# Which bursts of a unit hand a quarter of their exps to VectorE: 0, 2, 4, 6 in place of 1, 3, 5, 7

## The chip, the cores and the metric

The kernel runs on one core of a Trainium2 chip. The metric is the device time of one execution in microseconds; lower is better. The engines are called TensorE (PE in the profile, its weight loads PEld), ScalarE (ACT), VectorE (DVE), GpSimd (POOL) and SyncE (SP, which issues most DMAs).

## What is computed

Two branches over 2048 tokens of 1024 features, mixed by a gate for each token:

```python
g = sigmoid((A_x * gate_w).sum(-1, keepdims=True))
a = ssm(A_x)      # h_t = Lam_bar * h_(t-1) + B_bar x_t, complex; y = 2 Re(C h) + Dskip * x
b = mha(A_x)      # 32 heads of 32: softmax(q k^T / sqrt(32)) v, then @ wo
return g * a + (1 - g) * b
```

The attention branch takes 32 x 2048 x 2048 = 134 million exps, and these are what ScalarE does nearly all the time.

## The kernel before

The attention is cut into 512 **bursts**. A group is four heads (8 groups), a unit is 256 queries of a group (8 units a group), and a burst is 256 keys of a unit (8 bursts a unit, numbered 0 to 7). Bursts are also numbered through, from 0 to 511; burst 481 is burst 1 of unit 60.

In a burst TensorE makes the scores of four heads in PSUM (`burst`, L1575): eight matmuls, two PSUM slots of two banks each, out of three slots that rotate. The first slot holds heads 0 and 1, the second heads 2 and 3. ScalarE then runs one exp a slot, 128x1024 into a bf16 tile (L1593). Two bursts later TensorE multiplies these tiles with V (`pv`, L1649: 16 small matmuls a burst), which add up in bank 6 over a whole unit. With burst 1 of the next unit the sum is complete; VectorE divides by the row sums (`normalize`, L1662 and L1663) and a DMA transposes the result.

Everything else is poured into the bursts by hand-written rules in `build`: **dense chains** on TensorE of four matmuls a burst into bank 7. These are the projections of the next group (`proj`, `vproj`; L1402, L1420), the inputs of the state-space branch (`u`; L1432), its outputs (`c`; L1461 with a small diagonal matmul L1467 after every four), and at the end the output projection (`out`; L1492). When a chain is done, VectorE evacuates bank 7 (L1409, L1426, L1438, L1474, L1498). The next chain can't start before that, so in the burst in which a chain ends the value matmuls are placed behind the dense ones, except where the unit's sum is completed. VectorE also runs the scans and products of the state-space branch (L1340, L1349) in what time `build` reckons is left of each burst (`dve_t`, `limit`, `period`).

In some half-units **VectorE takes a quarter of the second slot's exps**: a pair of bursts of a half-unit, 256 columns each (the last head's scores for the second 128 keys). In a burst of a pair VectorE reads the columns at once, scales them to a fixed-point power of two and stores them as integers (x_in, L1584). ScalarE's second exp is then 128x768 (L1590); it is issued only after x_in is done, since the two share a bank. When both bursts of a pair are read, three steps on VectorE (x_q, L1614, L1615, L1611) work out a cubic for the fraction, and one on POOL (L1612) writes the bf16 bits, xp. TensorE multiplies xp with V in four small matmuls (`x_pv`, L1629), and the value group of such a burst has 14 matmuls instead of 16.

`X_PLAN` lists the half-units that have a pair, by the number of their first burst, and `X_AT` says which two bursts of a half-unit form it. `x_plan` (L1595) sets when L1629 is issued: in burst 6 for a pair of the first half, in burst 1 of the next unit for one of the second half, just ahead of that unit's `normalize`. In `build` the pair is planned at the half-unit's first burst (L1738); steps of an earlier pair that are left are put out before x_in of a new one (L1740), and the steps come ahead of other background work on VectorE. All queues run in the order in which `build` records their instructions.

The launch ends in a tail in which the last unit is finished without overlap.

Of the kernel before, what the change touches and what calls it, by code (L numbers as in the profile page):

```python
# [931 lines left out]
RING = 60  # L932
C_LOADS = 28

X_AT = ((1, 3), (5, 7))
X_PLAN = (144, 148, 152, 156, 160, 164, 168, 172, 176, 180, 184, 188, 192, 196, 200, 204, 208, 212, 216, 220, 224, 228, 232, 236, 240, 244, 248, 252, 256, 260, 296, 300, 304, 308, 312, 316, 320, 324, 352, 360, 364, 368, 372, 376, 380, 392, 396, 400, 404, 408, 412, 416, 420, 424, 428, 432, 436, 440, 444, 448, 452, 456, 460, 464, 468, 472, 476, 480, 484, 488, 492, 496, 500)
X_COLS = 256
X_A = SCALE * math.log2(math.e) * 65536.0
X_LO = -127.0 * 65536.0
# [14 lines left out]
class FastPath:  # L954
# [722 lines left out]
    def build(self):  # L1677
# [54 lines left out]
        for p in range(first, NBURST):  # L1732
# [3 lines left out]
            if p > first:  # L1736
                t0 += period
            if p % 4 == 0 and p in X_PLAN:  # L1738
                self.x_plan(p // 8, X_AT[p // 4 % 2])
            while p in self.x_of and len(self.xbg) > 1:  # L1740
# [315 lines left out]
```

## Time and profile before

| | |
|---|---|
| median of 3 runs | 944.16 us (943.36 to 944.33) |
| the profiled execution | 945.17 us, its span 943.3 us |
| TensorE busy | 912.6 us (97%), weight loads 506.8 us (54%) |
| ScalarE busy | 919.3 us (97%) |
| VectorE busy | 714.6 us (76%) |
| GpSimd busy | 57.1 us (6%) |
| mean granted TensorE clock | 0.996 |
| bursts with an exp on VectorE | 146 (73 pairs) |

Rows of a timeline give the start in us, the time in us, the engine, the line, the operation, what it writes and reads, and how many instructions of the kind were merged; in brackets, how long the engine sat idle before and what ended it. A row of the waits gives the waiting instruction, what it waited for, the sum in us, how often, and the longest. A unit of eight bursts lasts some 14 us.

### The profile page before, as it was taken

The numbers are of one execution on the slowest core, as the hardware profiler recorded it, in microseconds if no ns is written. First come the engines' busy times: TensorE is split into PE (matmuls) and PEld (weight loads), VectorE is DVE, ScalarE is ACT, GpSimd is POOL, SyncE is SP. The second block draws the span as 40 slices with busy tenths as digits, with TensorE's granted clock in tenths as the row PEclk, the third lists the DMA queues.
The fourth block names the chain that finished last, engine by engine and source line by source line (L and its number), as shares of the span: only waits on it lengthen the run. The fifth ranks groups of instructions, "written<-read, shape, count | busy, mean of one in ns | idle before, by whom it ended". The sixth has DMA issues, their size and how long they took to land.

```text
span 943.3 us, 33875 instructions
## 1 busy us (share of the span) xinstructions
PE 912.6 (97%) x15316; PEld 506.8 (54%) x15316; DVE 714.6 (76%) x1462; ACT 919.3 (97%) x1034; POOL 57.1 (6%) x113
## 2 busy tenths in 40 slices
PE   8899999999999999999999999999999999999996
PEld 4555644565455565455655555544655655554553
DVE  2788888899888888885679965468989755576664
ACT  6999999999999999999999999999999999999996
POOL 2000000000000001010010010000000001001000
PEclk9999999999999999999999999999999999999998
DMA  9559533310123002121022401124101111424312
GB/s 197 96 105 133 75 55 78 77 31 26 41 64 94 19 8 50 41 72 42 8 38 53 85 16 41 41 61 97 42 16 41 42 38 52 151 85 122 116 61 73
DMA packets 157093, 60.90 MB, mean 65 GB/s; under 512 B 145680, under 2 KB 145680, under 8 KB 156944
## 3 DMA queue, kind: packets, MB, share of 16 engines
q1 hardware_dynamic: 154784, 58.16, 27.7%
q8 instruction: 121, 1.98, 0.9%
q10 hardware_dynamic: 2160, 0.53, 0.3%
q14 instruction: 28, 0.23, 0.1%
HBM read 16.79 MB, written 12.58 MB: 31 GB/s over the span
## 4 chain that ended last, share of the span: by engine, by line
ACT 48%; PE 42%; DVE 5%; POOL 1%; SPq 1%; DMA 1%; issue 1%; DVEq 0%
ACT f_pt L1593 40%; PE f_ps L1649 9%; PE f_ps L1461 9%; PE f_ps L1575 8%; PE f_ps L1402 4%; PE f_ps L1492 4%; PE f_ps L1420 3%; ACT f_OT L1593 2%; PE f_ps L1432 2%; ACT f_Et L1593 2%; ACT f_cT_re L1593 2%; ACT f_cT_im L1593 2%; ACT f_pt L1590 1%; DVE f_xq L1611 1%; POOL f_xp L1612 1%; DVE f_xq L1615 1%
## 5 line engine op out<-in xcount | busy, mean ns | idle before, releaser
L1593 ACT ACTIVATE f_pt<-f_ps 128x1024 bf16<-128x1024 f32 x798 | 753.9, 1138 | 8.4 <-PE f_ps L1575 7.0
L1649 PEld LDWEIGHTS f_ps<-f_V,f_pt 128*128 128x128 bf16 x7260 | 223.9, 96 | 95.6 <-issue 67.9
L1649 PE MATMUL f_ps<-f_V,f_pt 128*128 128x33 bf16 x7260 | 259.8, 178 | 0.0
L1575 PE MATMUL f_ps<-f_Q,f_K 32*128 32x256 bf16 x4096 | 203.5, 273 | 13.9 <-ACT f_pt L1593 2.8
L1575 PEld LDWEIGHTS f_ps<-f_Q,f_K 32*128 32x128 bf16 x4096 | 60.8, 92 | 153.1 <-ACT f_pt L1593 119.9
L1584 DVE TENSOR_SCALAR f_xi<-f_ps 128x256 int32<-128x256 f32 x146 | 61.8, 424 | 101.7 <-PE f_ps L1575 99.0
L1432 PE MATMUL f_ps<-f_xT,f_wb 128*128 128x512 bf16 x512 | 131.4, 378 | 0.6 <-DVE f_pf L1223 0.4
L1590 ACT ACTIVATE f_pt<-f_ps 128x768 bf16<-128x768 f32 x146 | 125.2, 857 | 0.0
L1402 PE MATMUL f_ps<-f_xT,f_wb 128*128 128x512 bf16 x464 | 119.4, 379 | 0.0
L1612 POOL TENSOR_SCALAR f_xp<-f_xq 128x512 int16<-128x512 f32 x73 | 47.7, 654 | 629.3 <-DVE f_xq L1611 629.3
L1349 DVE TENSOR_TENSOR_SCAN f_ht<-f_pf,f_init,f_ut 128x512 bf16<-128x512 f32 x64 | 80.5, 1273 | 0.0
L1461 PE MATMUL f_ps<-f_cT_re,f_hp 128*128 128x512 bf16 x192 | 72.7, 379 | 0.0
L1461 PE MATMUL f_ps<-f_cT_im,f_hp 128*128 128x512 bf16 x192 | 72.6, 378 | 0.0
L1492 PE MATMUL f_ps<-f_wb,f_OT 128*128 128x512 bf16 x220 | 62.9, 381 | 0.1
L1432 PEld LDWEIGHTS f_ps<-f_xT,f_wb 128*128 128x128 bf16 x512 | 40.1, 96 | 39.2 <-issue 7.8
L1420 PE MATMUL f_ps<-f_wb,f_xT 128*128 128x128 bf16 x896 | 59.3, 219 | 0.0
L1402 PEld LDWEIGHTS f_ps<-f_xT,f_wb 128*128 128x128 bf16 x464 | 36.1, 96 | 36.5 <-issue 8.2
L1420 PEld LDWEIGHTS f_ps<-f_wb,f_xT 128*128 128x128 bf16 x896 | 50.4, 97 | 3.8 <-issue 3.6
L1611 DVE SCALAR_TENSOR_TENSOR f_xq<-f_xi,f_xq 128x512 f32<-128x512 int16 x73 | 50.5, 692 | 2.5
L1614 DVE SCALAR_TENSOR_TENSOR f_xq<-f_xi 128x512 f32<-128x512 uint16 x73 | 50.4, 690 | 2.0
L1615 DVE SCALAR_TENSOR_TENSOR f_xq<-f_xq,f_xi 128x512 f32<-128x512 f32 x73 | 50.0, 685 | 0.9
L1438 DVE CAST f_ub<-f_ps 128x512 bf16<-128x512 f32 x48 | 33.1, 690 | 15.5 <-PE f_ps L1432 15.2
(147 smaller groups left out, 841.6 us busy)
## 6 DMA issues: line engine op xcount, KB each, us to landing
ag_scratch<-f_Ag SPq DMA_DIRECT2D x32, 256.0 KB, 2.2
f_hp<-ag_scratch SPq DMA_DIRECT2D x32, 256.0 KB, 2.9
f_wb<-in_B_wqkv_dram SPq DMA_DIRECT2D x21, 256.0 KB, 4.0
out_dram<-f_xT SPq DMA_DIRECT2D x16, 256.0 KB, 2.2
f_wb<-in_B_wo_dram SPq DMA_DIRECT2D x2, 768.0 KB, 6.1
f_OT<-f_On SPq DMA_TRANSPOSE x63, 2.3
f_wb<-in_B_wqkv_dram ACTq DMA_DIRECT2D x2, 256.0 KB, 4.1
f_wb<-in_A_B_re_dram SPq DMA_TRANSPOSE x32, 3.4
```

The source lines that it names most:

```text
L1349: ops.append((1.29, lambda ri=ri: dve(lambda e: e.tensor_tensor_scan(ht[:, ri, :], rr, ut[:, ri, :], self.init[:, ri, j:j + 1], ALU.mult, ...
L1402: mms.append((1, lambda e, f, l, a=a: e.matmul(ps[:, bank, :], w[:, g % 2, part, a, :], xT[:, a, 512 * ch:512 * (ch + 1)], start=f, stop=l ...
L1420: m = e.matmul(ps[:, bank, 128 * q:128 * (q + 1)], xT[:, a, 128 * kt:128 * (kt + 1)], w[:, g % 2, 2, a, :], start=(a == 0), stop=(a == 7))
L1432: mms.append((1, lambda e, f, l, a=a: e.matmul(ps[:, 7, :], bT[:, (2 * n + ri) % 3, a, :], xT[:, a, 512 * ch:512 * (ch + 1)], start=f, sto ...
L1461: mms.append((1, lambda e, f, l, j=j, ri=ri: e.matmul(ps[:, 7, :], hp[:, ri, j, cols], cT[ri][:, j, 512 * cb:512 * (cb + 1)], start=f, sto ...
L1492: mms.append((1, lambda e, f, l, j=j: e.matmul(ps[:, 7, :], OT[:, j, 256 * qb + 128 * r:256 * qb + 128 * (r + 1)], wo[j][0][:, 512 * cb:51 ...
L1575: m = e.matmul(ps[:, 2 * sl[h // 2] + h % 2, 256 * kl:256 * (kl + 1)], K[32 * h:32 * h + 32, g % 2, 128 * kt:128 * (kt + 1)], Q[32 * h:32 ...
L1584: first = self.dve(lambda e: e.tensor_scalar(self.xi[:, X_COLS * n:X_COLS * (n + 1)], ps[:, 2 * s + 1, 512 - X_COLS:512], X_A, X_LO, ALU.m ...
L1590: self.S.op("act", lambda e, s=s, p=p: e.activation(flat(self.tile[p]), flat(ps[:, 2 * s:2 * s + 2, :]), ACT.Exp, scale=SCALE), reads=[("S ...
L1593: self.act(lambda e, s=s, p=p: e.activation(self.tile[p], ps[:, 2 * s:2 * s + 2, :], ACT.Exp, scale=SCALE), [("S", s)], [("pt", p)], "exp")
L1611: self.dve(lambda e: e.scalar_tensor_tensor(xq[:], hi, 128.0 / X_K, xq[:], ALU.mult, ALU.add), i2 + ["xq"], ["xq"], "x_q")
L1649: m = e.matmul(ps[:, 6, o:o + 33], self.tile[p][:, h2, 256 * kl + 128 * qt:256 * kl + 128 * (qt + 1)], V[:, g % 2, 2 * i + kl, h, :], star ...
```

## The change

The pairs of a half-unit are bursts 0 and 2, or 4 and 6, instead of 1 and 3, or 5 and 7. The list of half-units is drawn anew by the same rule: 144, 352 and 376 drop out, 328 and 332 come in, so 72 pairs are left of 73.

```diff
-X_AT = ((1, 3), (5, 7))
-X_PLAN = (144, 148, 152, ..., 320, 324, 352, 360, 364, 368, 372, 376, 380, 392, ..., 500)
+X_AT = ((0, 2), (4, 6))
+X_PLAN = (148, 152, ..., 320, 324, 328, 332, 360, 364, 368, 372, 380, 392, ..., 500)
```

No other line changes. L1596, by which L1629 is issued in burst 6 or in burst 1 of the next unit, stays as it is. What `build` records changes with the two tables: x_in, the shorter exps and the 14-matmul value groups move by one burst. Around them the order on VectorE changes. Of the 73 last x_q steps before, 62 were followed at once by the next x_in; of the 72 after, 13 are, and 52 are followed by the evacuation of a dense chain. C chains shift by two bursts around bursts 198 and 402, and with them their stores.

More of the change, by code (lines that the diff above doesn't have):

```diff
@@ L933 @@
 C_LOADS = 28
-X_AT = ((1, 3), (5, 7))
-X_PLAN = (144, 148, 152, 156, 160, 164, 168, 172, 176, 180, 184, 188, 192, 196, 200, 204, 208, 212, 216, 220, 224, 228, 232, 236, 240, 244, 248, 252, 256, 260, 296, 300, 304, 308, 312, 316, 320, 324, 352, 360, 364, 368, 372, 376, 380, 392, 396, 400, 404, 408, 412, 416, 420, 424, 428, 432, 436, 440, 444, 448, 452, 456, 460, 464, 468, 472, 476, 480, 484, 488, 492, 496, 500)
+X_AT = ((0, 2), (4, 6))
+X_PLAN = (148, 152, 156, 160, 164, 168, 172, 176, 180, 184, 188, 192, 196, 200, 204, 208, 212, 216, 220, 224, 228, 232, 236, 240, 244, 248, 252, 256, 260, 296, 300, 304, 308, 312, 316, 320, 324, 328, 332, 360, 364, 368, 372, 380, 392, 396, 400, 404, 408, 412, 416, 420, 424, 428, 432, 436, 440, 444, 448, 452, 456, 460, 464, 468, 472, 476, 480, 484, 488, 492, 496, 500)
 X_COLS = 256
```

## The prediction

> **What bounds the kernel now.** I read the page first: ScalarE and TensorE are both busy 97% of the span, and the chain that ended last changes hands between them.
>
> ```profile
> span 943.3 us, 33875 instructions
> ...
> PE 912.6 (97%) x15316; PEld 506.8 (54%) x15316; DVE 714.6 (76%) x1462; ACT 919.3 (97%) x1034; POOL 57.1 (6%) x113
> ...
> ACT 48%; PE 42%; DVE 5%; POOL 1%; SPq 1%; DMA 1%; issue 1%; DVEq 0%
> ```
>
> So the stages have to be told apart. In a burst without an exp on VectorE the score matmuls (L1575) start 1.83 us apart and are released by ScalarE, here in the timeline of the weight loads:
>
> ```profile
> 507.06 0.12 PEld L1575 LDWEIGHTS f_ps<-f_Q,f_K 32*128 32x128 bf16 x8 [0.56 <-ACT f_pt L1593]
> 508.89 0.12 PEld L1575 LDWEIGHTS f_ps<-f_Q,f_K 32*128 32x128 bf16 x8 [0.55 <-ACT f_pt L1593]
> ```
>
> The same timeline of unit 60 (bursts 480 to 487, VectorE's exps in 481, 483, 485 and 487), one L1575 row a burst, and two rows of ScalarE in it:
>
> ```profile
> 876.33 0.12 PEld L1575 LDWEIGHTS f_ps<-f_Q,f_K 32*128 32x128 bf16 x8
> 876.65 0.47 PEld L1649 LDWEIGHTS f_ps<-f_V,f_pt 128*128 128x128 bf16 x16 [0.21 <-issue]
> ...
> 878.03 0.12 PEld L1575 LDWEIGHTS f_ps<-f_Q,f_K 32*128 32x128 bf16 x8 [0.42 <-ACT f_pt L1593]
> 878.36 0.41 PEld L1649 LDWEIGHTS f_ps<-f_V,f_pt 128*128 128x128 bf16 x14 [0.21 <-issue]
> 879.02 0.17 PEld L1629 LDWEIGHTS f_ps<-f_V,f_xp 128*128 128x128 bf16 x4 [0.25 <-POOL f_xp L1612]
> ...
> 880.10 0.12 PEld L1575 LDWEIGHTS f_ps<-f_Q,f_K 32*128 32x128 bf16 x8 [0.42 <-ACT f_pt L1593]
> ...
> 881.98 0.12 PEld L1575 LDWEIGHTS f_ps<-f_Q,f_K 32*128 32x128 bf16 x8 [0.42 <-ACT f_pt L1593]
> ...
> 883.62 0.12 PEld L1575 LDWEIGHTS f_ps<-f_Q,f_K 32*128 32x128 bf16 x8
> ...
> 885.32 0.12 PEld L1575 LDWEIGHTS f_ps<-f_Q,f_K 32*128 32x128 bf16 x8 [0.42 <-ACT f_pt L1593]
> ...
> 886.98 0.12 PEld L1575 LDWEIGHTS f_ps<-f_Q,f_K 32*128 32x128 bf16 x8
> ...
> 888.79 0.12 PEld L1575 LDWEIGHTS f_ps<-f_Q,f_K 32*128 32x128 bf16 x8 [0.42 <-ACT f_pt L1593]
> ...
> 890.43 0.12 PEld L1575 LDWEIGHTS f_ps<-f_Q,f_K 32*128 32x128 bf16 x8
> ```
>
> ```profile
> 876.10 0.88 ACT L1590 ACTIVATE f_pt<-f_ps 128x768 bf16<-128x768 f32 x1
> ...
> 879.51 0.92 ACT L1590 ACTIVATE f_pt<-f_ps 128x768 bf16<-128x768 f32 x1
> 880.55 2.91 ACT L1593 ACTIVATE f_pt<-f_ps 128x1024 bf16<-128x1024 f32 x3
> ```
>
> The bursts last 1.70, 2.07, 1.88, 1.64, 1.70, 1.66, 1.81 and 1.64 us, 14.10 in all. Their differences are TensorE's work: 16 value matmuls against 14 cost 0.06 (rows 0.47 and 0.41), the matmuls on xp (L1629) 0.10. The gap of 0.42 before L1575 is the same wherever a dense chain's matmuls stand in front, so I read it as TensorE's own and not as ScalarE's. Two bursts stand out. Burst 1 (2.07) has less work than burst 6 (1.81) and is longer: in it L1629 waits 0.25 us for POOL's xp. Burst 2 (1.88) waits for the bank of the chain that ended in burst 1. ScalarE needs 3.41 us for three long exps and a short one (876.10 to 879.51, so 0.91 and 0.69 each), 13.6 a unit; it is within reach but not the limit. After the wait it idles: the short exp at 879.51 is followed only 1.04 later.
>
> The view of waits gives the sum of this wait; the timeline of VectorE and TensorE in burst 151 to 153 shows one of the long ones:
>
> ```profile
> PEld f_ps L1629 <- POOL f_xp L1612: 8.7, 22, 0.8
> ...
> PE f_ps L1629 <- POOL f_xp L1612: 5.2, 11, 0.7
> ```
>
> ```profile
> 287.78 0.40 PE L1575 MATMUL f_ps<-f_Q,f_K 32*128 32x256 bf16 x8
> ...
> 291.18 0.40 PE L1575 MATMUL f_ps<-f_Q,f_K 32*128 32x256 bf16 x8
> ...
> 292.68 0.27 PE L1629 MATMUL f_ps<-f_V,f_xp 128*128 128x33 bf16 x4 [0.66 <-POOL f_xp L1612]
> ...
> 293.81 0.40 PE L1575 MATMUL f_ps<-f_Q,f_K 32*128 32x256 bf16 x8
> ```
>
> ```profile
> 288.29 0.42 DVE L1584 TENSOR_SCALAR f_xi<-f_ps 128x256 int32<-128x256 f32 x1
> 289.18 0.69 DVE L1438 CAST f_OT<-f_ps 128x512 bf16<-128x512 f32 x1 [0.47 <-PE f_ps L1432]
> 289.79 0.68 DVE L1614 SCALAR_TENSOR_TENSOR f_xq<-f_xi 128x512 f32<-128x512 uint16 x1
> 290.50 0.69 DVE L1615 SCALAR_TENSOR_TENSOR f_xq<-f_xq,f_xi 128x512 f32<-128x512 f32 x1
> 291.23 0.69 DVE L1611 SCALAR_TENSOR_TENSOR f_xq<-f_xi,f_xq 128x512 f32<-128x512 int16 x1
> 292.01 0.62 POOL L1612 TENSOR_SCALAR f_xp<-f_xq 128x512 int16<-128x512 f32 x1 [6.22 <-DVE f_xq L1611]
> ```
>
> The second pair of a unit is read in burst 7, its three steps come after that burst's evacuation, and TensorE wants xp in burst 1 of the next unit: xp was there 4.9 us after burst 7's L1575 (287.78 to 292.68), and was wanted at 291.18 + 0.74 (the place of L1629 behind L1575 in burst 1, from 878.03 to 879.02 less its wait), 4.1 after it.
>
> **The change, part by part.** *Pairs one burst earlier, wanted when they were.* The offsets 6 and 9 in L1596 stay. From the rows: x_in starts 0.5 after L1575 and takes 0.42; the three steps follow at 0.71, 0.73 and 0.78; POOL takes 0.62 and L1629 starts 0.05 later: 3.8 us when nothing stands between. From burst 6's L1575 to the want is 1.81 + 1.64 + 1.70 + 0.74 = 5.9. So 2.1 us are left, and an evacuation (0.69) or a slow POOL (row below, 1.52) fits in them. The first pair gains a burst on a slack that already sufficed. All waits on xp go. Their worth: burst by burst, burst 1's length less that of the same work without the wait. The first is 2.63 (291.18 to 293.81) less 1.81 for its C work, 0.82; unit 60 gives 2.07 less 1.75 (burst 6 with 14 value matmuls), 0.32; the last (505) is another 0.32. There are 36 such bursts, 12.3 us together; the two rows of waits say 13.9, the upper end. I take **-12.3**.
>
> ```profile
> 406.95 1.52 POOL L1612 TENSOR_SCALAR f_xp<-f_xq 128x512 int16<-128x512 f32 x1 [5.10 <-DVE f_xq L1611]
> ```
>
> *The short value group moves into a covered burst.* Groups of 14 stood in bursts 1, 3, 5, 7; now in 0, 2, 4, 6. Burst 2 ends a fixed time after the evacuation of burst 1's chain, however short its value group: 0.06 is lost a unit. With 29 units whose chain ends in burst 1: **+1.6**.
>
> *Dense chains.* The recording's VectorE budget puts C chains two bursts off around bursts 198 and 402, so that more of them end in burst 1. The price of such an end, from the timeline:
>
> ```profile
> 565.14 0.40 PE L1575 MATMUL f_ps<-f_Q,f_K 32*128 32x256 bf16 x8
> ...
> 566.95 0.40 PE L1575 MATMUL f_ps<-f_Q,f_K 32*128 32x256 bf16 x8
> 567.06 0.75 DVE L1474 TENSOR_SCALAR f_Ag<-f_ps,f_gcol 128x512 f32<-128x512 f32 x1 [0.25 <-PE f_ps L1461]
> 567.40 2.96 ACT L1593 ACTIVATE f_pt<-f_ps 128x1024 bf16<-128x1024 f32 x3
> 567.87 0.39 PE L1461 MATMUL f_ps<-f_cT_re,f_hp 128*128 128x512 bf16 x1
> ...
> 568.89 0.40 PE L1575 MATMUL f_ps<-f_Q,f_K 32*128 32x256 bf16 x8
> ```
>
> Burst 2 then lasts 1.94 (566.95 to 568.89) instead of 1.76 with 16 value matmuls; four more of these make 4 x 0.18 = **+0.7**. The chain's store to scratch moves with it on SP's queue, past stores and transposes; the buffers are double and the stores are read far later, so it costs nothing.
>
> *One pair fewer* (bursts 144, 352 and 376 lose theirs, 328 and 332 gain one). Four plain bursts take 7.33; with a pair 6.81 (883.62 to 890.43), or 7.02 with the longer C work: **+0.4**. VectorE loses 2.9 us of work and POOL 0.6, both beside other work.
>
> *Where plain bursts follow.* Four of the 36 waits lie in half-units that stay or become plain, where ScalarE's 1.83 would take back part of what they free: of 1.7 us I put **+0.6**.
>
> *x_in behind the evacuation.* In the recorded order x_in stood behind the last x_q in 62 of 146 cases; now it stands behind an evacuation in 117 of 144. The worst case is the one above: the evacuation ends at 567.81, 0.86 after L1575, x_in would end at 1.30, and the short exp may start 0.91 after the exp at 567.40, that is 1.36 after L1575. Elsewhere the evacuation ends 0.3 earlier. It costs nothing, by a margin of 0.06 in burst 2. Then x_in and two steps follow in burst 2 and the third in burst 3, done some 3.4 after burst 2's L1575, or 1.5 into burst 3, about when that burst's chain ends; bounds 0 and 0.1 us a unit, and I take 0 since the value matmuls behind the chain cover the evacuation.
>
> Sum: -12.3 + 1.6 + 0.7 + 0.4 + 0.6 = **-9.0 us**. The profiled execution took 945.17, so 936.2 with a span near 934.3; it was 1.0 above the median 944.16, and against that the forecast is **935.2 us**. With 13.9 gone and only the pair lost it would be 930.7, the lower bound.
>
> **The rivals.** *The two engines meet.* Without the wait a unit of such work costs TensorE about 13.8 and ScalarE 13.6. If they hold each other up by 0.06 us in each of 72 half-units, 4.3 us are lost: 939.5. For it: the margin is 0.2 a unit. Against: in bursts 483 to 487 no such loss is seen.
>
> *Slower: the short exp waits for x_in.* If evacuations end later than in the rows above, x_in passes its 1.36 and ScalarE is late in every such burst. From 0.07 us later in all 144 bursts on (9 us) it eats the gain; at 0.17 beyond the margin the time would be 935.2 + 144 x 0.1 = 949.6. For it: the 0.06 of burst 2. Against: three bursts of four have 0.3 more, and where ScalarE is a little early TensorE sets the pace.
>
> *No change: ScalarE alone sets the time,* the waits on xp are covered, and what counts is its 0.44 us for the lost pair: 944.6. The idle at 880.55 speaks against it. The Trainium skill ("Perfetto Trace Analysis", Identifying the Most-Contended Engine) would have it so: it says that matmul busy time misleads, that TensorE's headroom is judged by the weight loads' share, and that the engine of highest occupancy is the one to work on. By that, 54% against ScalarE's 97%, the change brings nothing; the spacing of unit 60's bursts, which follows TensorE's work, disagrees.
>
> **How the numbers follow.** Forecast 0.68, the engines meet 0.17, slower 0.09, no change 0.06. A difference of 0.2% (1.9 us) is about what a measurement of this kernel can tell from no change. Faster: 0.68 + 0.17 = 0.85; same 0.06; slower 0.09. The range runs from the lower bound, rounded, 931.0, to just past the case where the engines meet, 940.0.
>
> **What would show it.** Right: the rows "L1629 <- POOL" gone from the waits; burst 1 near 1.81 where it was 2.0 to 2.6; POOL's op ending in burst 0 or before; ScalarE's short exp count at 144. Wrong: waits of L1590 on VectorE's L1584; evacuations that end over 0.9 after L1575; L1575 waiting longer for ScalarE inside the pair stretches; new waits of the first dense matmul on an evacuation in bursts 0, 4 or 6.

## The result, and the profile after

The changed kernel takes 939.07 us (median of 5 runs, 938.90 to 939.55) against 944.33 us of the kernel before (5 runs, 943.36 to 944.86): a ratio of 0.9946 [0.9931, 0.9960], so 5.3 us faster. The forecast was 935.2 us, 9.0 us faster. The sign and the main mechanism came as predicted; 3.7 us of the gain did not.

The page of the changed kernel: its span, the busy times, the chain that ended last, and the two groups of ScalarE's exps (the last column is ScalarE's idle time ahead of them).

```profile
span 937.3 us, 33936 instructions
...
PE 910.5 (97%) x15316; PEld 504.8 (54%) x15316; DVE 716.6 (76%) x1457; ACT 918.4 (98%) x1034; POOL 56.0 (6%) x112
...
ACT 53%; PE 41%; DVE 3%; SPq 1%; issue 1%; DMA 1%; DVEq 0%
...
L1593 ACT ACTIVATE f_pt<-f_ps 128x1024 bf16<-128x1024 f32 x800 | 755.2, 1154 | 2.9 <-PE f_ps L1575 2.2
...
L1590 ACT ACTIVATE f_pt<-f_ps 128x768 bf16<-128x768 f32 x144 | 125.0, 868 | 0.8 <-DVE f_xi L1584 0.7
```

The profiled execution took 939.07 us, the median itself. ScalarE's busy time is what it was (919.3 before); the span around it is 6.0 us shorter. POOL, 1% of the chain before, is gone from it. The view of the waits says why:

```profile
PEld f_ps L1575 <- ACT f_pt L1593: 129.1, 334, 1.0
...
DVE f_rc L1662 <- PE f_ps L1629: 47.7, 34, 2.3
...
ACT f_pt L1590 <- DVE f_xi L1584: 0.7, 1, 0.7
```

No row "L1629 <- POOL" is left, where two stood before: 8.7 us for the weight loads, 5.2 us for the matmuls. (They don't add up to 13.9 us of waiting: the 11 waits of the second row lie in bursts that the 22 of the first have too.) VectorE's `normalize` (L1662) waits longer for the value matmuls than before (47.7 us in sum against 15.3), since its own work is done earlier. A new row has come: ScalarE's short exp (L1590) waits for x_in (L1584), once, 0.7 us. The timeline of the weight loads in unit 60, one L1575 row a burst as in the prediction:

```profile
870.61 0.12 PEld L1575 LDWEIGHTS f_ps<-f_Q,f_K 32*128 32x128 bf16 x8
870.94 0.41 PEld L1649 LDWEIGHTS f_ps<-f_V,f_pt 128*128 128x128 bf16 x14 [0.21 <-issue]
...
872.38 0.12 PEld L1575 LDWEIGHTS f_ps<-f_Q,f_K 32*128 32x128 bf16 x8 [0.54 <-ACT f_pt L1593]
872.70 0.47 PEld L1649 LDWEIGHTS f_ps<-f_V,f_pt 128*128 128x128 bf16 x16 [0.21 <-issue]
873.10 0.17 PEld L1629 LDWEIGHTS f_ps<-f_V,f_xp 128*128 128x128 bf16 x4
...
874.18 0.12 PEld L1575 LDWEIGHTS f_ps<-f_Q,f_K 32*128 32x128 bf16 x8 [0.42 <-ACT f_pt L1593]
...
876.07 0.12 PEld L1575 LDWEIGHTS f_ps<-f_Q,f_K 32*128 32x128 bf16 x8 [0.42 <-ACT f_pt L1593]
...
877.76 0.12 PEld L1575 LDWEIGHTS f_ps<-f_Q,f_K 32*128 32x128 bf16 x8
...
879.43 0.12 PEld L1575 LDWEIGHTS f_ps<-f_Q,f_K 32*128 32x128 bf16 x8 [0.44 <-ACT f_pt L1593]
...
881.12 0.12 PEld L1575 LDWEIGHTS f_ps<-f_Q,f_K 32*128 32x128 bf16 x8
...
882.88 0.12 PEld L1575 LDWEIGHTS f_ps<-f_Q,f_K 32*128 32x128 bf16 x8 [0.43 <-ACT f_pt L1593]
...
884.57 0.12 PEld L1575 LDWEIGHTS f_ps<-f_Q,f_K 32*128 32x128 bf16 x8
```

The bursts now last 1.77, 1.80, 1.89, 1.69, 1.67, 1.69, 1.76 and 1.69 us, 13.96 in all instead of 14.10. Burst 1 fell from 2.07 to 1.80, and L1629 follows the value matmuls with no idle time. But burst 0 grew from 1.70 to 1.77 although its value group is the short one now, and the gap in front of the next L1575 is 0.54 instead of 0.42. POOL's op was done 2.2 us before L1629 wanted it:

```profile
870.30 0.62 POOL L1612 TENSOR_SCALAR f_xp<-f_xq 128x512 int16<-128x512 f32 x1 [6.01 <-PE f_ps L1492]
```

**A measure for what follows.** The spacing of the L1575 rows cuts the run into bursts. All that differs between the kernels lies between L1575 of burst 144 and that of burst 508: 275.39 to 926.00 us before, 274.78 to 919.75 after, so 650.61 and 644.97 us. This stretch became 5.6 us shorter. The start of burst 144 lies between 274.40 and 275.46 in all the kernels below, with no order to it, so the 0.6 us ahead of the stretch are left out. In every profile the granted clock is 1.00 over the whole stretch, and lower behind it (0.76 in the last 17.6 us of the changed kernel), so what the clock does to the end of the launch doesn't touch this measure either. It comes from one profiled execution a kernel.

### The profile page after: what moved, and what is told of

It reads as the page before. It is cut to its first block, busy times and chain, and to the rows that moved or that the text cites. A ratio compares the mean times of both kernels' runs of the same rounds, so it can differ in the third digit from the quotient of the medians.

```text
span 937.3 us, 33936 instructions
## 1 busy us (share of the span) xinstructions
PE 910.5 (97%) x15316; PEld 504.8 (54%) x15316; DVE 716.6 (76%) x1457; ACT 918.4 (98%) x1034; POOL 56.0 (6%) x112
## 4 chain that ended last, share of the span: by engine, by line
ACT 53%; PE 41%; DVE 3%; SPq 1%; issue 1%; DMA 1%; DVEq 0%
ACT f_pt L1593 44%; PE f_ps L1649 10%; PE f_ps L1461 9%; PE f_ps L1575 8%; PE f_ps L1492 4%; PE f_ps L1402 4%; PE f_ps L1420 3%; PE f_ps L1432 2%; ACT f_OT L1593 2%; ACT f_pt L1590 2%; ACT f_Et L1593 2%; ACT f_cT_re L1593 2%; ACT f_cT_im L1593 2%; SPq L1052 1%; DVE f_Ag L1474 1%
## 5 line engine op out<-in xcount | busy, mean ns | idle before, releaser
L1593 ACT ACTIVATE f_pt<-f_ps 128x1024 bf16<-128x1024 f32 x800 | 755.2, 1154 | 2.9 <-PE f_ps L1575 2.2
L1575 PE MATMUL f_ps<-f_Q,f_K 32*128 32x256 bf16 x4096 | 203.4, 273 | 16.2 <-ACT f_pt L1593 3.3
L1575 PEld LDWEIGHTS f_ps<-f_Q,f_K 32*128 32x128 bf16 x4096 | 60.7, 92 | 158.7 <-ACT f_pt L1593 129.1
L1590 ACT ACTIVATE f_pt<-f_ps 128x768 bf16<-128x768 f32 x144 | 125.0, 868 | 0.8 <-DVE f_xi L1584 0.7
L1584 DVE TENSOR_SCALAR f_xi<-f_ps 128x256 int32<-128x256 f32 x144 | 60.7, 421 | 26.8 <-PE f_ps L1575 24.8
L1662 DVE RECIPROCAL f_rc<-f_ps 128x8 f32<-128x8 f32 x63 | 13.1, 207 | 63.8 <-PE f_ps L1629 47.7
```

The lines of the kernel that those rows point to most:

```text
L1575: m = e.matmul(ps[:, 2 * sl[h // 2] + h % 2, 256 * kl:256 * (kl + 1)], K[32 * h:32 * h + 32, g % 2, 128 * kt:128 * (kt + 1)], Q[32 * h:32 ...
L1584: first = self.dve(lambda e: e.tensor_scalar(self.xi[:, X_COLS * n:X_COLS * (n + 1)], ps[:, 2 * s + 1, 512 - X_COLS:512], X_A, X_LO, ALU.m ...
L1590: self.S.op("act", lambda e, s=s, p=p: e.activation(flat(self.tile[p]), flat(ps[:, 2 * s:2 * s + 2, :]), ACT.Exp, scale=SCALE), reads=[("S ...
L1593: self.act(lambda e, s=s, p=p: e.activation(self.tile[p], ps[:, 2 * s:2 * s + 2, :], ACT.Exp, scale=SCALE), [("S", s)], [("pt", p)], "exp")
```

## The experiments

Times are medians. The kernel before gave 943.90 us beside the first four kernels, on the same chip, and 944.18 beside the last two, on another.

### The new list alone

```diff
-X_PLAN = (144, 148, 152, ..., 324, 352, 360, 364, 368, 372, 376, 380, ..., 500)
+X_PLAN = (148, 152, ..., 324, 328, 332, 360, 364, 368, 372, 380, ..., 500)
 X_AT = ((1, 3), (5, 7))
```

> The kernel before with the changed list of 72 half-units, pairs still at 1, 3 and 5, 7. If the position is what gains: the waits of L1629 on POOL stay near 14 us and the time is that of the kernel before plus the lost pair, 944.3 + 0.4 = 944.7 (944.0 to 945.5). If the new list brings part of the gain: 942 or less.

Measured: 944.49 us, ratio 1.0004 [0.9995, 1.0013]; the stretch 650.87 us, 0.3 longer. Its waits:

```profile
PEld f_ps L1629 <- POOL f_xp L1612: 9.0, 25, 0.8
...
PE f_ps L1629 <- POOL f_xp L1612: 5.3, 15, 0.7
```

The waits on xp are all there. The gain comes from the places of the pairs, not from the list.

### No wait, nothing else moved

```diff
-            self.dve(lambda e: e.scalar_tensor_tensor(xq[:], hi, 128.0 / X_K, xq[:], ...), ..., "x_q")
...
-                (0.7, 0.0, lambda: self.dve(lambda e: e.scalar_tensor_tensor(xq[:], xq[:], E1 / E3 * w * w, lo, ...), ..., "x_q")),
+                (0.7, 0.0, lambda: None),
```

The base is the kernel before, with its pairs and its order; xp is ready two steps earlier. The edit also takes 97 us of work off VectorE (busy 618.0 us against 714.6).

> The kernel before with two of the three x_q steps (L1615, L1611) left out, the recorded order otherwise the same; the cubic is then not computed, only its first step. xp is there 1.4 us earlier and no wait in burst 1 was longer than 0.8. If those waits are what the change removes: 12.3 us less some 1.5 us that ScalarE takes back, 933.5 (932.5 to 936), with burst 1 at 1.75 to 1.81. If ScalarE alone sets the time: 944. If the waits only cost half of what the rows say: 938 to 939.

Measured: 933.73 us, ratio 0.9891 [0.9876, 0.9906]; no row "L1629 <- POOL"; the stretch 640.00 us. So the waits were worth 10.6 us (10.2 by the medians), not 12.3, if VectorE's lighter load does nothing else; the table below bears on that. The chain that ended last, on its page, and burst 0 and 1 of unit 60 in the timeline of the weight loads:

```profile
ACT 96%; SPq 1%; DVE 1%; DMA 1%; PE 1%; issue 0%; DVEq 0%
```

```profile
866.90 0.12 PEld L1575 LDWEIGHTS f_ps<-f_Q,f_K 32*128 32x128 bf16 x8
...
868.61 0.12 PEld L1575 LDWEIGHTS f_ps<-f_Q,f_K 32*128 32x128 bf16 x8 [0.42 <-ACT f_pt L1593]
...
870.36 0.12 PEld L1575 LDWEIGHTS f_ps<-f_Q,f_K 32*128 32x128 bf16 x8 [0.42 <-ACT f_pt L1593]
```

Burst 0 lasts 1.71 and burst 1 1.75 us, the number that the prediction had put for this work without the wait. ScalarE now carries 96% of the chain: without the waits the two engines stand so close that the chain runs almost wholly through ScalarE. Where the 10.6 us come from is seen when the bursts of the stretch are summed by their place in the unit (364 bursts, in us; worked out from all L1575 rows):

| burst of the unit | 0 | 1 | 2 | 3 | 4 | 5 | 6 | 7 | sum |
|---|---|---|---|---|---|---|---|---|---|
| before | 80.60 | 94.19 | 84.14 | 77.61 | 78.13 | 76.95 | 82.44 | 76.55 | 650.61 |
| without the wait | 80.54 | 82.52 | 83.79 | 78.42 | 78.33 | 77.40 | 82.43 | 76.57 | 640.00 |
| changed kernel | 80.60 | 83.57 | 85.06 | 80.83 | 77.73 | 78.04 | 80.83 | 78.31 | 644.97 |

Burst 1 gives 11.7 us, in 32 units, every one with a pair just before; no other burst gets more than 0.04 us shorter but bursts 2 and 4 of units 56 and 57, whose bursts 3 and 5 get longer by about as much. So it is the wait that counts here, not VectorE's load. About 1.1 are given back at once in bursts 2 to 5. Of these 0.7 lie in units 33, 41, 48 and 63, where plain bursts follow (unit 33: bursts 3 to 5 go from 1.69, 1.75, 1.81 to 1.83, 1.84, 1.83, ScalarE's own pace).

### The two casts put behind x_in

In the changed kernel two evacuations of the output chains (L1498) are followed by two casts on VectorE (L1504, L1505), in bursts 454 and 458, and x_in of these bursts stands behind all three. The timeline of VectorE in burst 458, then ScalarE's short exp, then the weight loads of bursts 458 to 460:

```profile
831.51 0.75 DVE L1498 SCALAR_TENSOR_TENSOR f_Et<-f_ps,f_gcol,f_hp 128x512 f32<-128x512 f32 x1
832.29 0.43 DVE L1504 CAST f_Et<-f_Et 128x512 bf16<-128x512 f32 x1
832.75 0.69 DVE L1505 TENSOR_TENSOR f_Et<-f_Et 128x512 bf16<-128x512 f32 x1
833.36 0.42 DVE L1584 TENSOR_SCALAR f_xi<-f_ps 128x256 int32<-128x256 f32 x1
```

```profile
833.82 0.81 ACT L1590 ACTIVATE f_pt<-f_ps 128x768 bf16<-128x768 f32 x1 [0.70 <-DVE f_xi L1584]
```

```profile
831.40 0.12 PEld L1575 LDWEIGHTS f_ps<-f_Q,f_K 32*128 32x128 bf16 x8 [0.42 <-ACT f_pt L1593]
...
833.28 0.12 PEld L1575 LDWEIGHTS f_ps<-f_Q,f_K 32*128 32x128 bf16 x8 [0.42 <-ACT f_pt L1593]
...
835.59 0.12 PEld L1575 LDWEIGHTS f_ps<-f_Q,f_K 32*128 32x128 bf16 x8 [0.86 <-ACT f_pt L1593]
```

x_in ends at 833.78, 2.38 us after its burst's L1575; the short exp starts 0.04 later, after 0.70 of idle time; burst 459 lasts 2.31 us. Burst 454 is the same with less: x_in ends 1.85 us after its burst's L1575. The three x_q steps that follow are late too, and with them the next evacuation, for which the first dense matmuls of bursts 456 and 460 wait. For burst 456, VectorE and the weight loads:

```profile
828.04 0.74 DVE L1498 SCALAR_TENSOR_TENSOR f_Et<-f_ps,f_gcol,f_hp 128x512 f32<-128x512 f32 x1
```

```profile
828.84 0.55 PEld L1492 LDWEIGHTS f_ps<-f_wb,f_OT 128*128 128x128 bf16 x4 [0.34 <-DVE f_Et L1498]
```

The edit puts the casts into VectorE's background work; in the trace they then come behind x_in of bursts 456 and 460:

```diff
-                    self.dve(lambda e: e.tensor_copy(hi, su), ...)
-                    self.dve(lambda e: e.tensor_tensor(lo, su, hi, ALU.subtract), ...)
+                    self.bg.append((0.45, lambda: self.dve(lambda e: e.tensor_copy(hi, su), ...), 0))
+                    self.bg.append((0.7, lambda: self.dve(lambda e: e.tensor_tensor(lo, su, hi, ALU.subtract), ...), 0))
```

> The changed kernel with the two casts of the last unit's sums (L1504, L1505) recorded as background work behind the next x_in instead of between the evacuation and x_in. If x_in late behind them is what lengthens bursts 452 to 460: the half-units from 452 to 463, now 7.11, 7.84 and 7.19, come to about 6.9 each, 1.4 us less, 937.6 (937.2 to 938.2), and the wait of L1590 on L1584 is gone. If those bursts are long for another reason (the loads of scratch, the shorter chains): 939.1.

Measured: 937.84 us, ratio 0.9936 [0.9922, 0.9949]; the stretch 643.68 us, 1.3 less than the changed kernel's. The same place, VectorE and the weight loads of bursts 458 to 460:

```profile
831.10 0.75 DVE L1498 SCALAR_TENSOR_TENSOR f_Et<-f_ps,f_gcol,f_hp 128x512 f32<-128x512 f32 x1
831.77 0.41 DVE L1584 TENSOR_SCALAR f_xi<-f_ps 128x256 int32<-128x256 f32 x1
```

```profile
831.02 0.12 PEld L1575 LDWEIGHTS f_ps<-f_Q,f_K 32*128 32x128 bf16 x8 [0.45 <-ACT f_pt L1593]
...
832.87 0.12 PEld L1575 LDWEIGHTS f_ps<-f_Q,f_K 32*128 32x128 bf16 x8 [0.42 <-ACT f_pt L1593]
...
834.47 0.12 PEld L1575 LDWEIGHTS f_ps<-f_Q,f_K 32*128 32x128 bf16 x8 [0.15 <-ACT f_pt L1593]
```

Burst 459 is 1.60 us again. The evacuation ahead of burst 456's chain starts 0.42 us before that burst's L1575, where it started 0.29 behind it, and the weight loads of bursts 456 and 460 no longer wait for it. For burst 456:

```profile
827.14 0.75 DVE L1498 SCALAR_TENSOR_TENSOR f_Et<-f_ps,f_gcol,f_hp 128x512 f32<-128x512 f32 x1
```

```profile
828.24 0.55 PEld L1492 LDWEIGHTS f_ps<-f_wb,f_OT 128*128 128x128 bf16 x4
```

The half-units that begin with bursts 452, 456 and 460 go from 7.11, 7.84 and 7.20 us to 6.91, 6.91 and 6.98, 1.35 together, and the wait of L1590 on L1584 is gone. Of these 1.35 us, 0.9 lie in bursts 455 and 459, which wait for a short exp that x_in made late: the mechanism of the slower rival, at two places. The other 0.44 lie in bursts 456 and 460, which wait for the late evacuation.

### Less for ScalarE in burst 7

```diff
+            elif z == 1 and i == 7 and B - 1 in self.x_of:
+                flat = lambda ap: ap.rearrange("p h n -> p (h n)")[:, 0:896]
+                self.act(lambda e, s=s, p=p: e.activation(flat(self.tile[p]), flat(ps[:, 2 * s:2 * s + 2, :]), ...), ...)
```

The base is the changed kernel; burst 7 is plain there, and its second exp gets 896 columns in place of 1024.

> The changed kernel with ScalarE's second exp of burst 7 cut to 896 columns in units whose second half has a pair (128 columns of exps are left out, about 0.11 us each). If ScalarE sets burst 0, which lasts 1.76 in units of 16-matmul chains where TensorE's work is 1.65: burst 0 falls to 1.65 to 1.68 there, 12 to 15 units by 0.1, 937.8 (937.3 to 938.3). If burst 0 is long for a reason on TensorE or VectorE: 939.1.

Measured: 936.91 us, ratio 0.9926 [0.9912, 0.9940]; the stretch 643.26 us, 1.7 less than the changed kernel's. That is more gain than expected: the time lies below the range. Burst 480 (burst 0 of unit 60) in the timeline of the weight loads:

```profile
869.01 0.12 PEld L1575 LDWEIGHTS f_ps<-f_Q,f_K 32*128 32x128 bf16 x8
...
870.66 0.12 PEld L1575 LDWEIGHTS f_ps<-f_Q,f_K 32*128 32x128 bf16 x8 [0.43 <-ACT f_pt L1596]
```

It lasts 1.65 us instead of 1.77, and the gap behind it is 0.43 again. Burst by burst the two kernels differ in burst 0 of 17 units, by 0.04 to 0.12, and hardly elsewhere. So in these units ScalarE, not TensorE, ends burst 0 of the changed kernel. Its rows there:

```profile
868.69 0.89 ACT L1590 ACTIVATE f_pt<-f_ps 128x768 bf16<-128x768 f32 x1
869.38 2.94 ACT L1593 ACTIVATE f_pt<-f_ps 128x1024 bf16<-128x1024 f32 x3
872.10 0.93 ACT L1590 ACTIVATE f_pt<-f_ps 128x768 bf16<-128x768 f32 x1
```

Three long exps and a short one take it 3.41 us, as before the change, while TensorE asks 1.69 + 1.65 = 3.34 us for bursts 7 and 0. This suggests why it is burst 0: the plain burst 7, with three exps in a row, now stands in front of the burst with the least work on TensorE.

### Only burst 7 moved

```diff
-X_AT = ((1, 3), (5, 7))
+X_AT = ((1, 3), (5, 6))
```

The base is the kernel before, with the list of the changed one. Only the last exp of a unit's second pair moves, one burst ahead; the other three pair bursts stay.

> The kernel before with the changed list of 72 half-units, and of all exps on VectorE only those of burst 7 moved, to burst 6: pairs at 1, 3 and 5, 6. If what gains is that the second pair is complete a burst earlier: no wait of L1629 on POOL, burst 1 at 1.81 in units of 16-matmul chains and 1.86 with C work, and a time below the changed kernel, since ScalarE has no short exp in burst 0 to be late with and the short value groups stand in bursts 0, 3, 5 and 7: 944.5 less 10.6 plus some 1.5, 935.5 (934.5 to 937). If each pair's move brings its part of the 5.4 us: 941 to 942. If the move of the first pair is what gains: 944.5.

Measured: 936.74 us, ratio 0.9926 [0.9912, 0.9939]; the stretch 643.53 us. No row "L1629 <- POOL" in its waits, and the weight loads of unit 60, bursts 0 and 1:

```profile
869.31 0.12 PEld L1575 LDWEIGHTS f_ps<-f_Q,f_K 32*128 32x128 bf16 x8
...
871.03 0.12 PEld L1575 LDWEIGHTS f_ps<-f_Q,f_K 32*128 32x128 bf16 x8 [0.49 <-ACT f_pt L1593]
...
871.75 0.17 PEld L1629 LDWEIGHTS f_ps<-f_V,f_xp 128*128 128x128 bf16 x4
...
872.86 0.12 PEld L1575 LDWEIGHTS f_ps<-f_Q,f_K 32*128 32x128 bf16 x8 [0.45 <-ACT f_pt L1593]
```

One exp moved by one burst takes away all waits on xp. By the median it is, with the next kernel, the fastest here that computes the whole reference: its slowest run (937.79) is below the fastest of the changed kernel (938.90). But the two were run at different times, and the intervals overlap, so its lead of some 2 us over the changed kernel is likely rather than shown; in the stretch it is 1.4 us. The expected reason for a lead did not hold: burst 0 lasts 1.72 us with its short value group and the gap behind it is 0.49, so ScalarE is late there too. The lead is nearly all the casts: the changed kernel with the casts moved has 643.68 us, 0.15 more than this one. It does not reach the kernel without the wait, for the most part in burst 1, which lasts 1.83 in place of 1.75, since its value group has 16 matmuls now and burst 0 the short one.

The same with the casts put behind x_in, as above:

```diff
-X_AT = ((1, 3), (5, 7))
+X_AT = ((1, 3), (5, 6))
...
+                    self.bg.append((0.45, lambda: self.dve(lambda e: e.tensor_copy(hi, su), ...), 0))
```

> The same with the two casts of the last unit's sums (L1504, L1505) as background work behind the next x_in. Here only one evacuation with casts (burst 453) stands ahead of an x_in (burst 454), where the changed kernel had three of them in the way. If x_in behind the casts costs what the changed kernel's rows say for burst 454, some 0.3 to 0.5 us: 935.1. If nothing: as move7to6.

Measured: 936.92 us, ratio 0.9928 [0.9914, 0.9941]; the stretch 643.33 us, 0.2 less. One half-unit gains 0.19 us (452: 6.98 to 6.79). So with the pairs at these places the casts cost about 0.2 us, less than expected, and the medians don't show it. (The expectation counts three evacuations with casts in the changed kernel; its trace has two, in bursts 454 and 458.)

Pairs in bursts 4 and 6 with 1 and 3 kept, or 0 and 2 with 5 and 7, were not tried: two pairs would then follow in adjacent bursts, and x_in of the next would overwrite the integers that the last step of the one before still reads (`build` puts out all steps but the last ahead of x_in).

## Why the prediction was right, and where it was off

The stretch from burst 144 to 507 gives the ledger (us). The forecast's terms are set against what the runs showed. Each run gives its item by itself; that they add up is taken for granted, and the row above the sum is what remains.

| step of the prediction | forecast | measured | by |
|---|---|---|---|
| waits on xp gone, with what plain bursts take back | -12.3 + 0.6 | -10.6 | run without the wait |
| one pair fewer, other list | +0.4 | +0.3 | run with the new list |
| x_in behind the evacuation, and the three steps behind x_in | 0 | +1.3 | run with the casts moved |
| ScalarE in burst 0 | 0 | +1.7 | run with less in burst 7 |
| four more C chains that end in burst 1 | +0.7 | +0.6 | lengths of burst 2 |
| short value group in a covered burst | +1.6 | +1.1 | what is left; lengths of burst 2 give 0.9 |
| sum | -9.0 | -5.6 | 644.97 - 650.61 |

**The waits: right in kind, 1.1 us too large.** All are gone, burst 1 stands at 1.80 to 1.87 wherever a pair came before it, but for the two units with the casts (the forecast said near 1.81), and xp is ready 2.2 us early where 2.1 was worked out. In burst 153, where the wait was 0.66 us, the weight loads and POOL's op of the pair before now read:

```profile
290.85 0.12 PEld L1575 LDWEIGHTS f_ps<-f_Q,f_K 32*128 32x128 bf16 x8 [0.32 <-ACT f_pt L1593]
...
291.57 0.17 PEld L1629 LDWEIGHTS f_ps<-f_V,f_xp 128*128 128x128 bf16 x4
...
292.71 0.12 PEld L1575 LDWEIGHTS f_ps<-f_Q,f_K 32*128 32x128 bf16 x8 [0.26 <-ACT f_pt L1593]
```

```profile
288.79 0.72 POOL L1612 TENSOR_SCALAR f_xp<-f_xq 128x512 int16<-128x512 f32 x1 [102.17 <-DVE f_xq L1611]
```

Burst 153 lasts 1.86 us instead of 2.63. The term went by burst 1 alone, and there 11.7 us were to be had. Its upper end of 13.9 us added two rows that list the same waits; that did not enter the forecast but set the lower bound of the range. The term lacked what the next bursts take back: 1.1 us, of which 0.7 in the four places named (0.6 was put), and the rest chiefly in bursts 5, where ScalarE is a little late once it no longer gets the pause of the wait (unit 23: 1.66 to 1.73).

**x_in behind the evacuation: the step that failed.** It said "It costs nothing, by a margin of 0.06", and took one evacuation of 0.75 us as the worst that can stand in front. In two bursts of the 117 the evacuation brings two casts of 0.43 and 0.69 us with it, x_in ends 2.38 us after L1575 where 1.36 was allowed, and three half-units lose 1.3 us together. About 0.9 of it is the late exp. The rest belongs to the next sentences of that paragraph, which put the three x_q steps at nothing "since the value matmuls behind the chain cover the evacuation": behind the casts they did not, and TensorE waited 0.34 us for it in each of two bursts. The count had been made of evacuations, not of what else the same function puts on VectorE's queue. The other places bore the step out: the view lists one wait of L1590 on L1584 in 144 exps. (The prices of the slower rival don't agree with each other either: 144 x 0.1 us stands for x_in 0.1 us beyond the margin, not 0.17.)

**The two engines: the rival was partly right.** It put 0.06 us on each of 72 half-units, 4.3 us, and so came to 939.5; the time came out close to that, but by other items in good part. What was found is 1.7 us, about 0.1 a unit in 17 units, all in burst 0. In the sum this stood at nothing, and it is the largest item that the sum missed. The forecast had looked for such a loss in bursts 483 to 487, and there it is small indeed; it had not asked where in the unit three long exps would meet the shortest stretch of TensorE's work once the pairs moved.

**C chains as sized, short groups a little less.** Six units have the longer burst 2 (1.91 to 1.95 instead of 1.76) and two lost it (1.94 to 1.71): +1.1 - 0.5 = 0.6. A short group in burst 2 gains nothing: unit 60 has 1.89 with 14 matmuls and 1.88 with 16, while burst 6 falls from 1.81 to 1.76. In 17 units burst 2 stays the same to 0.02 us in this way, which makes 0.9 us at 0.05 each; the forecast had 29 units (and 29 x 0.06 is 1.7, not 1.6). TensorE now waits at that place for the evacuation, in the timeline of the weight loads of the changed kernel:

```profile
861.14 0.55 PEld L1492 LDWEIGHTS f_ps<-f_wb,f_OT 128*128 128x128 bf16 x4 [0.17 <-DVE f_xT L1498]
```

The waits list no such row before the change. The 1.1 us of the table are only what remains of the sum; no run separates them.

**No change, because ScalarE alone sets the time: refuted.** The waits on xp were worth 10.2 us of the time while ScalarE was busy for 97%. The Trainium skill ("Perfetto Trace Analysis", Identifying the Most-Contended Engine) calls the engine of the highest occupancy the most contended and says to optimize it first, with TensorE judged by its weight loads or by its share of the peak arithmetic. From that the prediction drew that the change brings nothing; the run without the wait disagrees with what was drawn. Yet what remains once the waits are gone fits the rule: there ScalarE has 96% of the chain.

**The signs.** Gone rows, burst 1, POOL's end and 144 short exps came as named. Of the signs against, L1590 waiting on L1584 and L1575 waiting longer for ScalarE (0.54 at 872.38) both appeared, and they stand for 0.9 and 1.7 us, most of what the forecast missed. The fourth sign against came in two places: the first dense matmul waits for an evacuation in bursts 456 and 460 (0.34 each), behind the casts, and otherwise only in burst 2. That 939.07 lies so near to the 939.5 of the rival is luck in good part.

## What to carry to other kernels

Where an operand is late by a fixed distance, move the one step that makes it late: here one exp, one burst earlier, brought at least as much as moving all four. A wait on one of two nearly equal engines is worth its length less what the other one then asks for, so sum the following bursts too, and look where the second engine's longest run meets the first one's shortest. When an instruction is put behind another in a queue, list all that the other one's function issues, in each of its cases; two rare pairs of casts took 1.3 us here beside a gain of 5.3.

## What the runs showed of the hardware

- The idle time before L1575 tells who ends a burst, though the profile names ScalarE's L1593 as the releaser each time. Behind the dense chains of unit 60 it is 0.42 to 0.44 us where TensorE's own work sets the pace (it stays when ScalarE is given less to do), and 0.54 where ScalarE does (it falls to 0.43 then). The number to compare with depends on what stands in front: in unit 19 it is 0.32 us and falls to 0.26.
- ScalarE's mean time for the 128x1024 exp went from 1138 to 1154 ns when the waits went, with the same work in a shorter span. The row of the changed kernel stands in its page above; this is the one of the kernel before, where the number behind the comma is the mean time of one:

```profile
L1593 ACT ACTIVATE f_pt<-f_ps 128x1024 bf16<-128x1024 f32 x798 | 753.9, 1138 | 8.4 <-PE f_ps L1575 7.0
```

The exps start some 0.91 us apart (from 869.38 to 872.10 three of them in 2.72 us), so they overlap in the record. Neither the mean time nor the busy share of ScalarE (97% and 98%) tells how close it is to its limit; its idle time behind L1575, 7.0 us before and 2.2 after, does so better; it is 0.6 in the run without the wait, where ScalarE has 96% of the chain.
